# Banded attention and a Mish MLP on one core: VectorE's instructions in program order up to the end of the first product, the first chunk's weight words spread differently, and five buffers for a small store

## The chip, the cores and the metric

The kernel runs on one core of a Trainium2 chip. The metric is the device time of one execution in microseconds (us). Of the kernel before there are three runs: 1056.01 us in the median, from 1054.07 to 1056.55. The engines are TensorE (PE in the profile; PEld is its weight load), VectorE (DVE), ScalarE (ACT), GpSimd (POOL) and SyncE (SP, which only issues transfers). An engine takes its instructions in the order in which they were put into its queue.

## The reference

Two parts follow each other. The first is attention with a band: 8 batches, 8 heads, 576 positions, 64 values per head.

```python
scores = (q @ k.T) / sqrt(64)
bias = slope[h] * -abs(i - j)
mask = (i - j >= 0) and (i - j < 128)
scores = where(mask, scores + bias, -1e9)
attn = exp(scores - max(scores))
attn = attn / (sum(attn) + 1e-9)
x = attn @ v                     # laid out as 4608 tokens x 512
```

The second is an MLP on the 4608 tokens, with `w_in` of 512 x 2048 and `w_out` of 2048 x 512:

```python
h = x @ w_in
g = h * tanh(softplus(h))        # Mish
out = g @ w_out
```

The weights come as 64-bit floats; q, k and v are 32-bit.

## The kernel before

**The MLP.** It works in 9 chunks of 512 tokens (`c` = 0 to 8). Chunk `c` below 8 holds the first 512 positions of batch `c`; chunk 8 holds the last 64 positions of all 8 batches. For each chunk there is a first product and a second product. Both are carried out on numbers split into a high and a low part (`x` into two, the weights into two, `g` into two), with three matmuls for each pair. The first product is `first(c, j)` for `j` = 0 to 7: 24 matmuls with 512 columns into a PSUM tile `h`, and one Mish of ScalarE from `h` into a tile `g` in SBUF. Two successive `j` share one `g` tile, so that a new one is begun at every even `j`. The second product has 32 steps, `second(c, half, j, t)`, of 6 matmuls each; `parts` makes the high part `gh` (ScalarE) and the low part `gl` (GpSimd) of `g` for it.

**The attention.** Attention of batch `c + 1` is woven into the second product of chunk `c`; that of batch 0 comes before everything. For each of 4 pairs of heads there are two units (k = 0 to 7 in all), and beside each even unit a small one for the last 64 positions (`last_unit`, names that end in `l`). A unit goes through these steps, each with a place in the order: `scores` (TensorE, tile `s`), `exps` (VectorE adds the bias and finds the maximum, ScalarE takes the exponential and sums), `fold` (two halves of the band are added, 1e-9 is added to the sum, a reciprocal), `scale` (multiplication with the reciprocal), `weights` (TensorE transposes, VectorE multiplies by a mask and brings the result to SBUF; called the masked copy below), `values` (TensorE, tile `o`), `split_x` (ScalarE makes the high part of `x`, VectorE the low one). The last unit's `values` are copied to `xo` and stored to DRAM until chunk 8.

**The weight words.** `load_w` brings 16 tiles of raw 64-bit words to SBUF (8 of `w_in`, i0 to i7 here, 8 of `w_out`, o0 to o7), each as two halves of 512 words per partition. `convert_w` makes 32-bit numbers of a tile: for each half ScalarE copies into a PSUM tile `t` (named `ti` or `to` in the profile), three VectorE instructions work on `t` and the raw words, then ScalarE copies the high part into a split tile (`si`, `so`) and GpSimd subtracts to get the low part. The PSUM tiles `t` of the two halves lie in the banks `po0` and `po1`, which the second product uses later, or for the tiles made in the second product both in the bank `w`, one after the other; `w` is also the bank of the last unit's transposes (`pt_0l` and so on). Raw tiles, split tiles, the first attention inputs (`first`) and the `g` tiles come from one pool of 20 buffers (`big`). The last tile, o7, is loaded into the buffers of x2 and x3 once the first product of chunk 0 has read them.

**The order.** TensorE's and SyncE's instructions stay in the order in which the program issues them (`InOrder` with `fixed`). The order of VectorE, ScalarE and GpSimd is set ahead of time by a planner that steps through the program with its own costs and picks, for each engine, the earliest instruction of the program that it holds to be ready. So before the change words of the weights stand between the attention's instructions on VectorE, wherever the planner took VectorE to be free. `convert_next` is called three times within attention of batch 0 (at 3.6, 5.6 and 7.6 units), after each `first(0, j)` once or twice, and at every second step of the second product.

Of the kernel before, what the change touches and what calls it, by code (L numbers as in the profile page):

```python
# [8 lines left out]
F32 = mybir.dt.float32  # L9
# [3 lines left out]
AF = mybir.ActivationFunctionType  # L13
ALU = mybir.AluOpType

WINDOW = 128
P = 128
# [24 lines left out]
def attention_mish_mlp(  # L42
# [187 lines left out]
    def unit(b, p, half):  # L230
# [6 lines left out]
        st = {}  # L237
# [35 lines left out]

        def fold():
            sm, pz = st["sm"], st["pz"]
            two = pz if half else pz[:, 1:4:2]
            pool.tensor_tensor(out=two[:, :, :P], in0=two[:, :, :P], in1=two[:, :, P:], op=ALU.add)
            dve.tensor_scalar(out=sm, in0=sm, scalar1=1e-9, scalar2=None, op0=ALU.add)
            dve.reciprocal(sm, sm)

        def scale():
            (pool if b == 0 else dve).tensor_tensor(
                out=st["pz"][:, :, :P], in0=st["pz"][:, :, :P],
                in1=st["sm"].rearrange("p (c n) -> p c n", n=1).to_broadcast([P, 4, P]), op=ALU.mult,
            )

        def weights():
            pz = st["pz"]
# [44 lines left out]
    def last_unit(b, p):  # L333

        st = {}
        name = f"{b}_{p}l"

        def scores():
            qk, z = qkv[(b, p)]

            st["s"] = qkv[("s", b, p)][:, :, :96]
            for i in range(2):
                pe.matmul(
                    st["s"][:, i, :], lhsT=z, rhs=qk[:, 1, 384 + 96 * i : 480 + 96 * i],
                    start=True, stop=True,
                )

        def exps():
            mx = at.tile([P, 1], F32, tag="mxl", name=f"mx{name}")
            sm = st["sm"] = at.tile([P, 1], F32, tag="sml", name=f"sm{name}")  # L350
            pz = st["pz"] = at.tile([P, 192], F32, tag="pzl", name=f"pz{name}")
            dve.tensor_tensor_reduce(
                out=pz.rearrange("p (a n) -> p a n", a=2), in0=st["s"],
                in1=nl[:, p, :].rearrange("p (a n) -> p a n", a=2), scale=-SCALE, scalar=3.0e38,
                op0=ALU.add, op1=ALU.min, accum_out=mx,
            )
            act.activation(pz, pz, AF.Exp, bias=mx, scale=-1.0, accum_out=sm)

        def fold():
            sm, pz = st["sm"], st["pz"]  # L360
            dve.tensor_scalar(out=sm, in0=sm, scalar1=1e-9, scalar2=None, op0=ALU.add)
            dve.reciprocal(sm, sm)
            dve.tensor_tensor(out=pz[:, :64], in0=pz[:, :64], in1=pz[:, P:], op=ALU.add)
            dve.tensor_scalar(out=pz[:, :P], in0=pz[:, :P], scalar1=sm, scalar2=None, op0=ALU.mult)

        def weights():
            t = st["t"] = ps.tile([P, 512], F32, tag="w", name=f"pt{name}")
            pe.transpose(t[:, :P], st["pz"][:, :P], ident)
            pf = st["pf"] = at.tile([P, 2, 2, 64], F32, tag="pfl", name=f"pf{name}", bufs=1)
            shape = [P, 2, 2, 64]  # L370
            dve.tensor_tensor(
                out=pf, in0=t[:, :P].rearrange("p (u i n) -> p u i n", u=1, i=2).to_broadcast(shape),
                in1=masks[:, :, :64].rearrange("p u (i n) -> p u i n", i=1).to_broadcast(shape),
                op=ALU.mult,
            )

        def values():
            va, vl = qkv[("v", b, p)]
            o = st["t"][:, P : P + LEFT]
            for n, val in enumerate((va[:, 3, :], vl)):  # L380
                for i in range(2):
                    pe.matmul(
                        o[HEAD[i]], lhsT=val[:, HEAD[i]], rhs=st["pf"][:, n, i, :],
                        start=(n == 0), stop=(n == 1), skip_group_check=True,
                    )
            xo = at.tile([P, LEFT], F32, tag="xo", name=f"xo{name}")
            dve.tensor_copy(xo, o)
            sp.dma_start(out=xs[p, :, b * LEFT : (b + 1) * LEFT], in_=xo)

        return [  # L390
            (0.01, scores), (0.5, exps), (0.9, fold), (1.4, weights), (1.995, values),
        ]

# [113 lines left out]
        if conv and conv[0] in raw_w:  # L507
            convert_w(*conv.pop(0), tags)

    early = [(k, lambda: convert_next()) for k in (3.6, 5.6, 7.6)]  # L510
    for _, work in sorted(attention(0) + early, key=lambda s: s[0]):
        work()

    for c in range(B + 1):
        for j in range(NJ):
            if c == 0:
                while ("i", j) not in split:
                    convert_next()
            if j == NJ - 1:
                parts(c, 0, 0)  # L520
                parts(c, 0, 1)
            first(c, j)
            if c == 0:
                for _ in range(2 if j > 2 else 1):
                    convert_next()
        if c == 0:
            load_w(*last_w)

        n = 4 * NJ
        steps = []  # L530
        for m in range(2 * NJ):
# [2 lines left out]
            if m >= 2:  # L534
                steps.append((2 * m - 4.1, lambda m=m: parts(c, *divmod(m, NJ))))
            if c == 0:
                steps.append((2 * m + 0.5, lambda: convert_next(("w", "w"))))
        if c + 1 < B:
            steps += [((n - 2) / 9.0 * s - 0.2, f) for s, f in attention(c + 1)]
        elif c + 1 == B:  # L540
# [66 lines left out]
```

## Time and profile before

| what | value |
|---|---|
| median of three runs | 1056.01 us (1054.07 to 1056.55) |
| the profiled execution's own time | 1056.28 us |
| its span, first to last instruction | 1054.5 us |
| mean granted TensorE clock | 0.971 |
| busy: PE, PEld, DVE, ACT, POOL | 998.6, 787.4, 405.7, 391.5, 309.7 us |
| bytes moved | 59.32 MB |

The busy time of an engine is the sum of its instructions' time; for TensorE, whose matmuls are pipelined and whose ends are modelled, it says that there was work, not that it ran at its peak. The granted clock is that of TensorE as a share of 2.4 GHz: 1.00 is that level, 0.50 is 1.2 GHz. Of a timeline's line the columns are: start, duration, engine, operation, output and inputs, shapes, count of merged instructions, and in brackets how long the engine had been idle before and what ended that.

### The profile page before, as it was taken

Reading aid. Unit: us, or ns where it says so; the run is one execution under the profiler, and the core shown is the slowest. Engines: PE = TensorE matmul, PEld = TensorE weight load, DVE = VectorE, ACT = ScalarE, POOL = GpSimd, SP = SyncE. Lnnn points to the kernel's source line nnn. Section 1 sums busy time; section 2 is a strip of 40 time slices with the busy share of each in tenths; the row PEclk is TensorE's granted clock in tenths of the full one; section 3 lists DMA queues with packets and bytes.
Section 4 is the critical chain, followed back from the end, with each engine's and each line's share of the span. In section 5 each row is a group of like instructions: output and inputs, shape, how many; then the busy total and the mean of one; then the engine's idle time right before and its main releaser. Section 6 shows DMA issues by size and latency. Waiting matters only on the chain.

```text
span 1054.5 us, 14241 instructions
## 1 busy us (share of the span) xinstructions
PE 998.6 (95%) x5280; PEld 787.4 (75%) x5280; DVE 405.7 (38%) x1166; ACT 391.5 (37%) x926; POOL 309.7 (29%) x270
## 2 busy tenths in 40 slices
PE   4548989999999999999999999999999999999998
PEld 2336867787778877887778777877787778888886
DVE  4998067502760167106630564037501760000000
ACT  2544554323433345215422443235323442222221
POOL 3513754211431044004410342123311441041032
PEclk9567989999999999999999999999999999999999
DMA  8940022200220023002120032002100201000001
GB/s 269 399 159 13 1 66 91 70 1 20 64 71 32 1 62 93 33 1 60 58 68 1 25 93 68 1 24 85 58 21 1 71 25 41 20 21 21 1 1 40
DMA packets 52133, 59.32 MB, mean 56 GB/s; under 512 B 13024, under 2 KB 32608, under 8 KB 52064
## 3 DMA queue, kind: packets, MB, share of 16 engines
q1 hardware_dynamic: 50880, 57.69, 17.1%
q8 instruction: 42, 0.69, 0.3%
q10 hardware_dynamic: 1184, 0.72, 0.2%
q14 instruction: 27, 0.22, 0.1%
HBM read 47.91 MB, written 10.49 MB: 55 GB/s over the span
## 4 chain that ended last, share of the span: by engine, by line
PE 85%; DMA 4%; DVE 4%; issue 3%; POOL 2%; ACT 1%; SPq 0%; POOLq 0%; DVEq 0%
PE po L30 38%; PE h L30 33%; PE s L30 9%; PE o L30 5%; DMA wi<-in_moe_w_in_dram 2%; DMA wo<-in_moe_w_out_dram 1%; DVE pz L30 1%; POOL si L30 1%; DVE ti L30 1%; POOL so L30 1%; DVE to L30 1%; DMA nb<-in_relb_dram 1%; DVE wi L30 0%; SPq L30 0%; DMA first<-in_k_dram 0%
## 5 line engine op out<-in xcount | busy, mean ns | idle before, releaser
L30 PE MATMUL h<-x,si 128*128 128x512 f32 x1728 | 394.9, 390 | 0.0
L30 PEld LDWEIGHTS h<-x,si 128*128 128x128 f32 x1728 | 325.5, 188 | 68.0 <-issue 0.3
L30 PE MATMUL po<-so,gh 128*128 128x512 f32 x1152 | 324.8, 404 | 0.0
L30 POOL TENSOR_TENSOR gl<-g,gh 128x512 fp32r<-128x512 f32 x144 | 193.6, 1344 | 376.5 <-ACT gh L30 347.0
L30 PEld LDWEIGHTS po<-so,gh 128*128 128x128 f32 x1152 | 207.5, 189 | 48.6 <-ACT x L30 7.0
L30 DVE CUSTOM_DVE_ANT_0 pz<-s,nb 128x256 f32<-128x256 f32 (+1 forms) x256 | 84.6, 386 | 345.6 <-PE s L30 336.0
L30 PE MATMUL po<-so,gl 128*128 128x512 f32 x576 | 178.7, 391 | 0.0
L30 ACT ACTIVATE g<-h 128x1024 f32<-128x1024 f32 x72 | 74.0, 1028 | 268.8 <-PE h L30 268.8
L30 ACT ACTIVATE pz<-pz,mx 128x256 f32<-128x256 f32 (+1 forms) x256 | 120.3, 471 | 118.0 <-DVE mx L30 117.9
L30 POOL TENSOR_TENSOR pz<-pz 128x256 f32<-128x256 f32 x64 | 64.8, 1013 | 314.9 <-PE po L30 174.0
L30 ACT ACTIVATE gh<-g 128x512 fp32r<-128x512 f32 x144 | 90.6, 629 | 116.6 <-PE po L30 112.4
L30 PEld LDWEIGHTS po<-so,gl 128*128 128x128 f32 x576 | 108.6, 188 | 24.2
L30 DVE TENSOR_TENSOR pz<-s,masks 128x1024 f32<-128x1024 f32 x64 | 78.2, 1222 | 29.2 <-PE s L30 29.2
L30 DVE TENSOR_TENSOR pz<-pz,sm 128x512 f32<-128x512 f32 x56 | 61.9, 1106 | 11.0 <-POOL pz L30 8.9
L30 DVE COPY ob<-po 128x512 f32<-128x512 f32 x18 | 12.4, 692 | 124.9 <-PE po L30 124.9
L30 PE MATMUL s<-qk 64*128 64x128 f32 (+1 forms) x448 | 57.7, 376 | 0.0
L30 PE MATMUL o<-pz,va 128*64 128x128 f32 (+1 forms) x560 | 54.9, 325 | 0.0
L30 PEld LDWEIGHTS o<-pz,va 128*64 128x64 f32 x560 | 33.3, 136 | 27.8 <-issue 10.2
L30 ACT ACTIVATE x<-o 128x512 fp32r<-128x512 f32 x32 | 19.1, 598 | 83.8 <-PE o L30 83.8
L30 PE MATMUL o<-pz,first 128*64 128x128 f32 (+1 forms) x80 | 14.1, 517 | 36.0 <-DVE pz L30 36.0
L30 PE MATMUL s<-ident,pz 128*128 128x128 f32 x256 | 41.1, 286 | 7.4 <-POOL pz L30 4.3
L30 ACT ACTIVATION_READ_ACCUMULATOR pz<-pz,mx 128x1 f32 x256 | 47.8, 187 | 0.0
(114 smaller groups left out, 556.9 us busy)
## 6 DMA issues: line engine op xcount, KB each, us to landing
wi<-in_moe_w_in_dram SPq DMA_DIRECT2D x16, 512.0 KB, 10.4
wo<-in_moe_w_out_dram SPq DMA_DIRECT2D x16, 512.0 KB, 10.8
out_dram<-ob SPq DMA_DIRECT2D x32, 256.0 KB, 2.0
qk<-in_q_dram SPq DMA_DIRECT2D x28, 288.0 KB, 3.7
qk<-in_k_dram SPq DMA_DIRECT2D x28, 288.0 KB, 3.7
va<-in_v_dram SPq DMA_DIRECT2D x28, 256.0 KB, 2.9
first<-in_q_dram SPq DMA_DIRECT2D x4, 288.0 KB, 3.9
first<-in_k_dram SPq DMA_DIRECT2D x4, 288.0 KB, 4.4
```

Of the source, the lines that this page charges most:

```text
L30: ins = method(*args, **kwargs)
```

## The change

VectorE's instructions are kept in program order from the start until the first product of chunk 0 is issued (`dve.fixed`). Of the words of the weights only i0 is made within attention of batch 0 (at 7.0 units); after each `first(0, j)` two tiles are made as long as more than four are left, and the last four (o4 to o7) in the second product of chunk 0, at every step's half instead of every second one's. In all chunks `1e-9` is added by ScalarE. From batch 1 on `fold` and `scale` of a unit become one VectorE instruction for each column block with two halves (two in an even unit, four in an odd one), with a minimum's accumulator that nobody reads, and one ScalarE copy with a scale for each block with one half; GpSimd and the wide VectorE multiplication are no longer used there. In the last unit the addition and the multiplication of the first 64 columns become one VectorE instruction, and ScalarE scales the other 64. `xo` gets five buffers instead of two.

```diff
--- before.py
+++ after.py
@@ -273,16 +273,30 @@
 
         def fold():
             sm, pz = st["sm"], st["pz"]
-            two = pz if half else pz[:, 1:4:2]
-            pool.tensor_tensor(out=two[:, :, :P], in0=two[:, :, :P], in1=two[:, :, P:], op=ALU.add)
-            dve.tensor_scalar(out=sm, in0=sm, scalar1=1e-9, scalar2=None, op0=ALU.add)
+            if b == 0:
+                two = pz if half else pz[:, 1:4:2]
+                pool.tensor_tensor(out=two[:, :, :P], in0=two[:, :, :P], in1=two[:, :, P:], op=ALU.add)
+            act.activation(sm, sm, AF.Copy, bias=1e-9)
             dve.reciprocal(sm, sm)
 
         def scale():
-            (pool if b == 0 else dve).tensor_tensor(
-                out=st["pz"][:, :, :P], in0=st["pz"][:, :, :P],
-                in1=st["sm"].rearrange("p (c n) -> p c n", n=1).to_broadcast([P, 4, P]), op=ALU.mult,
-            )
+            sm, pz = st["sm"], st["pz"]
+            if b == 0:
+                pool.tensor_tensor(
+                    out=pz[:, :, :P], in0=pz[:, :, :P],
+                    in1=sm.rearrange("p (c n) -> p c n", n=1).to_broadcast([P, 4, P]), op=ALU.mult,
+                )
+                return
+
+            unread = at.tile([P, 4], F32, tag="un", name=f"un{name}")
+            for c in range(4):
+                if half or c % 2:
+                    dve.tensor_tensor_reduce(
+                        out=pz[:, c, :P], in0=pz[:, c, :P], in1=pz[:, c, P:], scale=sm[:, c : c + 1],
+                        scalar=3.0e38, op0=ALU.add, op1=ALU.min, accum_out=unread[:, c : c + 1],
+                    )
+                else:
+                    act.activation(pz[:, c, :P], pz[:, c, :P], AF.Copy, scale=sm[:, c : c + 1])
 
         def weights():
             pz = st["pz"]
@@ -358,10 +372,14 @@
 
         def fold():
             sm, pz = st["sm"], st["pz"]
-            dve.tensor_scalar(out=sm, in0=sm, scalar1=1e-9, scalar2=None, op0=ALU.add)
+            act.activation(sm, sm, AF.Copy, bias=1e-9)
             dve.reciprocal(sm, sm)
-            dve.tensor_tensor(out=pz[:, :64], in0=pz[:, :64], in1=pz[:, P:], op=ALU.add)
-            dve.tensor_scalar(out=pz[:, :P], in0=pz[:, :P], scalar1=sm, scalar2=None, op0=ALU.mult)
+            un = at.tile([P, 1], F32, tag="unl", name=f"un{name}")
+            dve.tensor_tensor_reduce(
+                out=pz[:, :64], in0=pz[:, :64], in1=pz[:, P:], scale=sm, scalar=3.0e38,
+                op0=ALU.add, op1=ALU.min, accum_out=un,
+            )
+            act.activation(pz[:, 64:P], pz[:, 64:P], AF.Copy, scale=sm)
 
         def weights():
             t = st["t"] = ps.tile([P, 512], F32, tag="w", name=f"pt{name}")
@@ -383,7 +401,7 @@
                         o[HEAD[i]], lhsT=val[:, HEAD[i]], rhs=st["pf"][:, n, i, :],
                         start=(n == 0), stop=(n == 1), skip_group_check=True,
                     )
-            xo = at.tile([P, LEFT], F32, tag="xo", name=f"xo{name}")
+            xo = at.tile([P, LEFT], F32, tag="xo", name=f"xo{name}", bufs=5)
             dve.tensor_copy(xo, o)
             sp.dma_start(out=xs[p, :, b * LEFT : (b + 1) * LEFT], in_=xo)
 
@@ -507,8 +525,9 @@
         if conv and conv[0] in raw_w:
             convert_w(*conv.pop(0), tags)
 
-    early = [(k, lambda: convert_next()) for k in (3.6, 5.6, 7.6)]
-    for _, work in sorted(attention(0) + early, key=lambda s: s[0]):
+
+    dve.fixed = True
+    for _, work in sorted(attention(0) + [(7.0, convert_next)], key=lambda s: s[0]):
         work()
 
     for c in range(B + 1):
@@ -521,10 +540,12 @@
                 parts(c, 0, 1)
             first(c, j)
             if c == 0:
-                for _ in range(2 if j > 2 else 1):
-                    convert_next()
+                for _ in range(2):
+                    if len(conv) > 4:
+                        convert_next()
         if c == 0:
             load_w(*last_w)
+            dve.fixed = False
 
         n = 4 * NJ
         steps = []
@@ -534,7 +555,7 @@
             if m >= 2:
                 steps.append((2 * m - 4.1, lambda m=m: parts(c, *divmod(m, NJ))))
             if c == 0:
-                steps.append((2 * m + 0.5, lambda: convert_next(("w", "w"))))
+                steps.append((m + 0.5, lambda: convert_next(("w", "w"))))
         if c + 1 < B:
             steps += [((n - 2) / 9.0 * s - 0.2, f) for s, f in attention(c + 1)]
         elif c + 1 == B:
```

## Rows read from the trace of the kernel before

**Rows 1.** Busy time by stage: start:end, length, engines, granted clock, DMA share, GB/s.

```profile
16.40:88.03 71.63, 34.84 (x204) 23.38 (x204) 66.28 (x169) 33.24 (x88) 22.01 (x20) 0.64 0.70 254
88.03:133.45 45.42, 45.42 (x194) 37.20 (x192) 13.08 (x22) 25.79 (x39) 29.54 (x24) 0.96 0.00 1
133.45:208.46 75.01, 70.75 (x422) 53.64 (x422) 49.81 (x140) 34.12 (x99) 33.25 (x27) 0.95 0.23 73
208.46:319.70 111.24, 111.24 (x614) 87.57 (x613) 44.22 (x134) 41.59 (x104) 29.66 (x24) 1.00 0.15 45
```

**Rows 2.** The chain of work that ended last: start, duration, what.

```profile
208.46 43.52 PE h L30 x192
...
1006.42 43.53 PE po L30 x192
```

**Rows 3.** TensorE's waits up to 135 us: total, times, longest.

```profile
PE o L30 <- DVE pz L30: 36.0, 8, 8.7
```

**Rows 4.** Timeline of TensorE in attention of batch 0 and behind it.

```profile
16.37 1.55 PE L30 MATMUL o<-pz,first 128*64 128x256 f32 x8 [1.26 <-DVE pz L30]
...
29.66 1.98 PE L30 MATMUL o<-pz,first 128*64 128x128 f32 x12 [8.65 <-DVE pz L30]
...
34.07 0.27 PE L30 MATMUL pt_1l<-ident,pz_1l 128*128 128x128 f32 x1
39.00 1.55 PE L30 MATMUL o<-pz,first 128*64 128x256 f32 x8 [4.66 <-DVE pz L30]
...
43.57 1.11 PE L30 MATMUL s<-ident,pz 128*128 128x128 f32 x4
...
88.03 45.49 PE L30 MATMUL h<-x,si 128*128 128x512 f32 x192
```

**Rows 5.** Timeline of VectorE up to the end of the first product.

```profile
28.40 1.21 DVE L30 TENSOR_TENSOR pz<-s,masks 128x1024 f32<-128x1024 f32 x1
...
91.80 1.30 DVE L30 TENSOR_SCALAR to<-to 128x512 uint32<-128x512 uint32 x2
...
94.20 1.28 DVE L30 SCALAR_TENSOR_TENSOR wo<-wo,to 128x512 uint32<-128x512 uint32 x2
```

**Rows 6.** Timeline of ScalarE: the first word, and the first product.

```profile
21.99 0.62 ACT L30 ACTIVATE ti<-wi 128x512 f32<-128x512 f32 x1 [5.74 <-DMA wi<-in_moe_w_in_dram]
...
95.48 1.03 ACT L30 ACTIVATE g<-h 128x1024 f32<-128x1024 f32 x1 [1.85 <-PE h L30]
96.40 2.31 ACT L30 ACTIVATE si<-wi 128x512 fp32r<-128x512 f32 x4
...
107.28 3.44 ACT L30 ACTIVATE si<-wi 128x512 fp32r<-128x512 f32 x6
```

**Rows 7.** Timeline of SyncE's queue: the first store of xo.

```profile
51.99 0.33 SPq L30 DMA_DIRECT2D xs<-xo_0l  x1
```

**Rows 8.** Timeline of GpSimd in the first product.

```profile
97.13 5.14 POOL L30 TENSOR_TENSOR si<-wi,si 128x512 fp32r<-128x512 f32 x4 [14.16 <-ACT si L30]
```

**Rows 9.** Timeline of ScalarE at the start of the second product.

```profile
136.38 0.62 ACT L30 ACTIVATE to<-wo 128x512 f32<-128x512 f32 x1 [1.65 <-DMA wo<-in_moe_w_out_dram]
```

**Rows 10.** Timeline of VectorE there: the last instruction of either half of o7.

```profile
138.50 0.69 DVE L30 SCALAR_TENSOR_TENSOR wo<-wo,to 128x512 uint32<-128x512 uint32 x1
...
147.67 0.68 DVE L30 SCALAR_TENSOR_TENSOR wo<-wo,to 128x512 uint32<-128x512 uint32 x1
```

**Rows 11.** Timeline of TensorE there.

```profile
146.26 1.09 PE L30 MATMUL s<-ident,pz 128*128 128x128 f32 x4 [3.12 <-DVE pz L30]
148.50 0.45 PE L30 MATMUL pt_0l<-ident,pz_0l 128*128 128x128 f32 x1 [1.14 <-DVE wo L30]
```

**Rows 12.** Timeline of VectorE in a later chunk: the multiplication of an odd unit.

```profile
375.57 1.45 DVE L30 TENSOR_TENSOR pz<-pz,sm 128x512 f32<-128x512 f32 x1
```

**Rows 13.** Timeline of TensorE there: the transposes of that unit.

```profile
379.90 0.60 PE L30 MATMUL s<-ident,pz 128*128 128x128 f32 x4
```

**Rows 14.** Busy time and granted clock behind a burst of TensorE (columns as in Rows 1).

```profile
54.00:56.00 2.00, 0.62 (x5) 0.38 (x3) 2.00 (x4) 0.56 (x1) 0.00 (x0) 0.98 1.01 404
```

## Prediction, made before the change was run

> **What bounds the kernel now.** I read the busy time by stage first, then the chain of waits, then TensorE's waits and the timelines of the first 210 us. From 208.46 us, where the first product of chunk 1 begins, TensorE is busy without a gap: 111.24 of 111.24 us in one whole chunk at clock 1.00 [rows 1], and the chain runs over TensorE's lines to the last product at 1006.42 [rows 2]. The change takes no matmul away, so these 1054.5 - 208.46 = 846.0 us stay as long as nothing makes TensorE wait there. What can move is the first 208.46 us, in three stages [rows 1]: attention of batch 0 (to 88.03; VectorE busy 66.28 of 71.63 us, TensorE 34.84, clock 0.64), the first product (45.42 us, TensorE full), and the second product with attention of batch 1 (75.01 us, against 111.24 - 43.52 = 67.7 us in a later chunk). In the first stage TensorE waits 36.0 us in 8 waits for VectorE's masked copies [rows 3]: its queue is a burst of `values`, `scores` and transposes of some 5 us, then nothing while VectorE works on weight words.
>
> **Attention of batch 0, words moved out.** In program order VectorE has only attention to do, so a masked copy follows as soon as the transposes are there. A burst lasts from 29.66 to 34.34 = 4.68 us behind an odd unit and from 39.00 to 44.68 = 5.68 us behind an even one [rows 4]; the masked copy adds 1.26 us until the next `values` (28.40 to 29.66) [rows 4, 5]. The cycles are 5.94 and 6.94 us where they now take about 10. From the first `values` at 16.37 [rows 4], four even and three odd cycles without the last one's scores: unit 6's `values` start at 16.37 + 3 x 6.94 + 3 x 5.94 = 55.0; 1.55 + 0.64 of those, 1.11 of transposes and 1.26 of masked copy give 59.5, unit 7's `values` (1.98) 61.5 us. Two things are added. The word i0 stands in unit 7's place on VectorE: 91.80 to 95.48 is 3.68 us for a tile [rows 5]; it lies mostly beside TensorE's burst, so 0 to 3.7 us, I take 1.5, as the burst is the longer. And ScalarE may take i0's copy when its data is not there yet, as it does now (5.74 us until 21.99) [rows 6]; the exponentials of unit 2 would stand behind it: 0 to 3.5 us, taken as 1. That is 64 us at the low clock of these rows. With all bursts at 1.00, half as long, the same sum gives about 51. One burst ended at 0.98 [rows 14], but the stage's mean was 0.64 [rows 1]; with pauses of 1.3 us in place of 5 it will be higher. I take 60: 28 us earlier than 88.03.
>
> The five `xo` buffers belong to this step: the first store leaves SyncE's queue only at 51.99, behind the weight loads [rows 7], and with two buffers the third copy to `xo`, now due near 40 us, would hold VectorE until then. I count the buffers as the removal of that wait and nothing more. SyncE's queue keeps its order.
>
> **The first product.** 192 matmuls, 45.42 us now [rows 1]. VectorE has 11 tiles behind attention, 11 x 3.68 = 40.5 us [rows 5], so it keeps ahead of 24 matmuls per 5.4 us on the whole. But only i0 is ready at the start. ScalarE's copies into split tiles come in groups behind every second Mish (96.40 behind 95.48, and six at 107.28) [rows 6], not when VectorE is done: buffers of a pool are handed out in program order, and `g` stands before the next split tiles. Before, three words were made ahead; after, i1 must wait for the first Mish. From the start of the product to that Mish 7.45 us, to the copy 0.92, to GpSimd 0.73, and 1.28 for a half [rows 4, 6, 8]: the low part of i1's first half is there after 10.4 us, of its second after 11.7, while TensorE is through with i0 at about 7.4 and can do 2 and then 4 more matmuls of 0.23. It waits 2.5 + 0.4 = 2.9 us; with 0.7 for the clock the stage is 49.0 us (bounds 43.5, all at 1.00 and no wait, and 52). It ends at 109.0 instead of 133.45.
>
> **The second product of chunk 0.** Here four tiles instead of one are made, in the one bank `w`, half behind half. A half takes 136.38 to 139.19 = 2.81 us from ScalarE's copy to VectorE's last instruction [rows 9, 10]. By the same program order the first small transposes `pt_0l` get the bank only behind all eight halves. VectorE ends its fixed list some 45 us after the product's start (1.3 for the last x, 40.5, and 3 of holds by ScalarE), 4 us before the second product; 8 x 2.81 = 22.5 us later, and 2 more for attention's own instructions between, the bank is free: 20.5 us into the second product. TensorE reaches `pt_0l` after 146.26 - 3.12 - 133.45 + 1.09 = 10.8 us [rows 1, 11]. It waits 9.7 us. Waits of 4.26 us cost 75.01 - 67.7 = 7.3 us before [rows 1, 11], so 3.0 of them were the low clock behind the wait; I add the same. Second product: 67.7 + 9.7 + 3.0 = 80.4 us (bounds: 67.7 if words are made early in VectorE's gaps, 91 with VectorE and ScalarE in turns). Chunk 1 starts at 189.4 instead of 208.46.
>
> **The cheaper fold and scale, and ScalarE's additions, in later chunks.** An odd unit's multiplication ends at 377.02 and its transposes start at 379.90 [rows 12, 13]: 2.9 us to spare. The new VectorE instruction with a scalar operand is not in the trace; four of them lie between a small part of 1.45 us and four times 1.45 [rows 12], I take 1.5 in all, since they read half the data each and one addition goes. ScalarE's added pieces are each under the 0.62 us of a 512-wide copy [rows 9]. GpSimd's addition before them goes. So 0 in either direction, hidden by TensorE's own work; if the 2.9 us were used up, the transposes would wait for the rest.
>
> **Sum.** 60 + 49.0 + 80.4 + 846.0 = 1035.4 us of span; the profiled execution took 1056.28 - 1054.5 = 1.78 us more than its span, so 1037.2 us. It lies 0.27 above the median of the runs, within their spread.
>
> **Rivals.** *The clock rises in attention of batch 0.* With pauses of 1.3 us the bursts run at 1.00 from the third on: the stage ends at 53, the first product takes 43.5 + 3, the second 80.4, chunk 1 starts at 179.9: 1027.7 us. For it speaks the 0.98 at the end of a burst [rows 14], against it that most bursts of the same length stayed low [rows 1]. The Trainium skill (TensorE: Matmul & The Clock Gate, Part 1) says that the throttled state is the default and that activity releases it; by that rule this rival is the likelier end of the range, and the trace agrees in that 1.00 stands in the later, gapless chunks.
>
> *Slower: the words in `w` hold TensorE far longer.* The two halves of o7 took from 136.38 to 148.35, 12.0 us, as attention's instructions got between them on VectorE [rows 9, 10]: 6.0 us per half. Eight at that pace end 43.9 us into the second product, TensorE waits 33.1 us, the stage takes 103.8 and chunk 1 starts at 212.8: 1060.6 us. It decides against the change from 5.4 us per half on. For it speaks that row; against it that TensorE, once it waits, brings VectorE no new attention work.
>
> *The change does not do what it says.* If ScalarE's or GpSimd's order, not VectorE's words, sets the 10 us cycle, attention ends at 88 as now and the added waits remain: 88 + 49.0 + 80.4 is 217.4, 1065 us. Against it: 66.28 of 71.63 us of VectorE are busy [rows 1].
>
> *Later chunks become bound by attention.* Four new instructions in a row that each wait for a GpSimd subtraction (1.28) [rows 8] cost 5.1 us, 2.2 beyond the 2.9 to spare, four times in each of 7 chunks: 62 us, 1099. From 0.7 us per odd unit on the gain is gone. Against it: GpSimd has 16 subtractions in a chunk, spaced by several us, so one or two can hit. The Trainium skill (SBUF — State Buffer, Who interferes with whom) says that a VectorE instruction with two SBUF inputs and a GpSimd instruction that reads SBUF exclude each other for their whole length; the 1.45 us in rows 12 are in line with it.
>
> **Chances.** Forecast 0.56 (its own range 1030 to 1045), clock 0.27, slow words 0.09, no release 0.05, later chunks 0.03. The range 1023 to 1048 leaves out the slower rivals and the far ends of the two stages' bounds. About 0.3% (3.2 us) is what can be told from no change: faster 0.85 (the first two and the near part of the third), same 0.03, slower 0.12.
>
> **What would show it.** Right: `h` starts near 60 us; VectorE has no weight word before unit 7; one wait of TensorE of some 3 us for GpSimd's `si` behind the first 24 matmuls; one of 5 to 15 us before `pt_0l`, released by VectorE's last word; the second product of chunk 1 as long as before. Wrong: `h` later than 70 us, more than one wait in the first product, or any wait of TensorE in later chunks.

## The result, and the profile after

The changed kernel takes 1043.57 us (median of 4, 1042.77 to 1045.11) where the kernel before took 1055.62 on the same chip: ratio 0.9889, 95% interval 0.9872 to 0.9907. It is faster, 12 us in the median; the forecast was 1037.2 us. The profiled execution has a span of 1043.4 us (before 1054.5) at a mean clock of 0.978.

Busy time by stage of the changed kernel, with the columns of [rows 1]: attention of batch 0, first product, second product with attention of batch 1, and chunk 1 as a whole.

```profile
16.48:65.61 49.13, 30.66 (x203) 21.22 (x204) 30.16 (x97) 22.64 (x78) 17.07 (x16) 0.77 0.98 363
65.61:122.39 56.78, 51.06 (x194) 40.36 (x193) 52.68 (x82) 36.96 (x58) 31.27 (x24) 0.87 0.02 6
122.39:197.18 74.79, 70.17 (x422) 53.09 (x421) 46.47 (x168) 41.73 (x127) 28.40 (x22) 0.95 0.24 73
197.18:308.57 111.39, 111.39 (x614) 87.72 (x613) 42.46 (x162) 46.52 (x128) 21.00 (x16) 1.00 0.15 44
```

Against [rows 1]: `h` starts 22.4 us earlier (65.61, before 88.03), the first product is 11.4 us longer (56.78, before 45.42), and the second and a later chunk are unchanged within 0.1 us. That is the 11.1 us of the span. (The 208.46 of [rows 1] and [rows 2], at which chunk 1 was taken to start, is a step of the chain of work; TensorE's timeline of the kernel before has the first `h` of chunk 1 at 208.30. The stages below go by the timelines; by them the last window above ends 0.16 us into chunk 2.) VectorE's load has moved from the first row (66.28 busy before, 30.16 now) to the second (13.08 before, 52.68 of 56.78 now).

TensorE's waits up to 100 us (total, times, longest); the line answers to [rows 3]:

```profile
PE o L30 <- DVE pz L30: 17.6, 8, 4.7
```

And its waits from 65 us to the start of chunk 1:

```profile
PE pt_0l L30 <- DVE wo L30: 3.9, 1, 3.9
PE h L30 <- ACT g L30: 3.4, 1, 3.4
PE h L30 <- ACT si L30: 1.7, 1, 1.7
PE s L30 <- ACT pz L30: 0.8, 1, 0.8
PE h L30 <- POOL si L30: 0.7, 1, 0.7
```

The second line was not forecast: in the first product TensorE waits for a Mish (`g`). The timeline of TensorE has it at 108.53, and the wait that answers to the second of [rows 11] at 137.55:

```profile
75.10 0.73 PE L30 MATMUL h<-x,si 128*128 128x512 f32 x2 [1.67 <-ACT si L30]
76.49 28.65 PE L30 MATMUL h<-x,si 128*128 128x512 f32 x118 [0.65 <-POOL si L30]
108.53 13.93 PE L30 MATMUL h<-x,si 128*128 128x512 f32 x48 [3.40 <-ACT g L30]
137.55 0.45 PE L30 MATMUL pt_0l<-ident,pz_0l 128*128 128x128 f32 x1 [3.87 <-DVE wo L30]
```

### The profile page after: what moved, and what is told of

It reads as the page before. It is cut to its first block, busy times and chain, and to the rows that moved or that the text cites. A ratio compares the mean times of both kernels' runs of the same rounds, so it can differ in the third digit from the quotient of the medians.

```text
span 1043.4 us, 14406 instructions
## 1 busy us (share of the span) xinstructions
PE 999.6 (96%) x5280; PEld 788.0 (76%) x5280; DVE 395.1 (38%) x1350; ACT 429.9 (41%) x1110; POOL 249.6 (24%) x214
## 4 chain that ended last, share of the span: by engine, by line
PE 89%; DMA 5%; DVE 2%; issue 1%; SPq 1%; ACT 1%; POOL 0%; POOLq 0%; DVEq 0%; ACTq 0%
PE po L30 38%; PE h L30 36%; PE s L30 9%; PE o L30 5%; DMA wi<-in_moe_w_in_dram 2%; DMA wo<-in_moe_w_out_dram 1%; SPq L30 1%; DMA xs<-xo_1l 1%; DVE ti L30 1%; DMA nb<-in_relb_dram 1%; DVE to L30 0%; PE pt_0l L30 0%; DVE wo L30 0%; PE pt_1l L30 0%; PE pt_3l L30 0%
## 5 line engine op out<-in xcount | busy, mean ns | idle before, releaser
L30 PE MATMUL h<-x,si 128*128 128x512 f32 x1728 | 400.6, 394 | 5.7 <-ACT g L30 3.4
L30 POOL TENSOR_TENSOR gl<-g,gh 128x512 fp32r<-128x512 f32 x144 | 188.1, 1307 | 709.5 <-ACT gh L30 682.1
L30 DVE CUSTOM_DVE_ANT_0 pz<-pz,sm 128x128 f32<-128x128 f32 x168 | 78.3, 511 | 1.2
L30 DVE TENSOR_TENSOR x<-o,x 128x512 fp32r<-128x512 f32 x32 | 22.1, 691 | 60.8 <-ACT x L30 60.8
L30 PEld LDWEIGHTS s<-ident,pz 128*128 128x128 f32 x256 | 32.6, 146 | 15.2 <-POOL pz L30 6.0
```

Source lines behind the costliest of these rows:

```text
L30: ins = method(*args, **kwargs)
```

## The experiments

Stages in us, read from one profiled execution of each kernel; ratio to the kernel before on the same chip, with its 95% interval. Several chips were used, on which the kernel before took 1055.03 to 1055.89 us in the median, so that medians of different rows compare to about 1 us. The code cuts leave out lines, at `...` and around them.

| kernel | median | ratio | `h` starts | first product | second product | chunk 1 starts |
|---|---|---|---|---|---|---|
| before | 1055.62 | 1 | 88.03 | 45.42 | 74.9 | 208.3 |
| after | 1043.57 | 0.9889 [0.9872, 0.9907] | 65.61 | 56.78 | 74.8 | 197.2 |
| order_only | 1046.77 | 0.9911 [0.9896, 0.9926] | 67.83 | 56.81 | 74.2 | 198.9 |
| fold_only | 1053.39 | 0.9980 [0.9970, 0.9989] | 84.75 | 45.37 | 74.9 | 205.0 |
| xo2 | 1055.39 | 0.9996 [0.9987, 1.0006] | 80.04 | 54.29 | 74.5 | 208.8 |
| words_held | 1057.97 | 1.0015 [1.0006, 1.0025] | 67.77 | 49.86 | 93.8 | 211.5 |
| held_13 | 1048.03 | 0.9932 [0.9915, 0.9948] | 66.10 | 54.13 | 81.7 | 201.9 |
| two_early | 1047.21 | 0.9921 [0.9907, 0.9936] | 67.30 | 54.25 | 77.0 | 198.5 |
| one_ahead | 1050.32 | 0.9954 [0.9939, 0.9968] | 67.27 | 58.34 | 77.2 | 202.8 |
| best | 1039.92 | 0.9859 [0.9844, 0.9874] | 67.08 | 56.38 | 69.2 | 192.7 |
| counts | 1044.66 | 0.9890 [0.9875, 0.9905] | 68.60 | 45.33 | 84.1 | 198.1 |
| best_pairs | 1052.32 | 0.9961 [0.9945, 0.9976] | 66.34 | 68.92 | 69.6 | 204.9 |
| tuned | 1051.26 | 0.9957 [0.9945, 0.9969] | 65.23 | 53.27 | 83.5 | 202.0 |
| last | 1038.27 | 0.9837 [0.9823, 0.9850] | 67.86 | 44.32 | 77.6 | 189.8 |

### The parts of the change: order_only, fold_only, xo2

order_only is the changed kernel with the old fold and scale; fold_only is the kernel before with the new ones.

```diff
-            act.activation(sm, sm, AF.Copy, bias=1e-9)
+            dve.tensor_scalar(out=sm, in0=sm, scalar1=1e-9, scalar2=None, op0=ALU.add)
...
-            for c in range(4):
...
+            (pool if b == 0 else dve).tensor_tensor(
```

> The changed kernel (1043.6 us) with fold, scale and the last unit's fold as they were before: only VectorE's order, the placing of the weight words and the five buffers are left of the change. Theory, the gain is all in the first 210 us and comes from the order: 1043.6, within 3 us, and every later chunk at 111.2 us. Rival, the cheaper fold and scale are part of the gain (GpSimd's addition and a 1.1 us multiplication per unit less): 1047 to 1053, with waits of TensorE in later chunks or a second product of chunk 0 that is longer by more than 3 us.

> The kernel before with the new fold, scale and last unit's fold alone (VectorE free to be ordered by the planner, words as before, two xo buffers). Theory, these parts are hidden in the later chunks and shorten only the chain of batch 0 by some 0.3 us per unit, which VectorE's words hide: within 2.5 us of before, 1053 to 1058 us. Rival, they are 2 to 3 us of the gain, as the difference of the run without them (1046.8) hints: 1050 to 1053 us.

Between before and fold_only lie 1.6 us in the medians (1055.03 on the same chip) and 3.3 us in the start of `h`. Between order_only and after lie 3.2 and 2.2 us, but their intervals overlap, and kernels with the same attention as the changed kernel's start `h` anywhere from 65.61 to 68.60 us (a table on this stands in the section on the prediction). The two of them with order_only's granted clock in that stage, 0.67, start it at 67.08 and 67.27, 0.6 to 0.8 us ahead of order_only. So the new fold gains something in attention of batch 0 (the last units' part and ScalarE's additions, as only these are new there), how much is not settled, and it changes nothing in later chunks, where neither kernel shows a wait of TensorE.

xo2 is the changed kernel with two `xo` buffers as before.

```diff
-            xo = at.tile([P, LEFT], F32, tag="xo", name=f"xo{name}", bufs=5)
+            xo = at.tile([P, LEFT], F32, tag="xo", name=f"xo{name}")
```

> The changed kernel with two buffers for xo in place of five. Theory, the buffers are a condition of the order: VectorE in program order reaches the third copy to xo near 45 us, but the first store is issued only near 52 us behind the weight loads and lands some 5 us later, so VectorE stands until 57 us, the first product starts near 77 us instead of 65.6, and the kernel takes 1053 to 1056 us. Rival, the store is early enough or VectorE has that time to spare: 1043 to 1045 us.

The whole gain is gone. The rows are from three timelines of xo2: SyncE issues the store of the first small copy at 52.21; VectorE's third small copy is held by that store, not until it is issued but until it has landed, 9 us later; and TensorE waits for the masked copy behind it.

```profile
52.21 0.33 SPq L30 DMA_DIRECT2D xs<-xo_0l  x1
```

```profile
61.37 0.22 DVE L30 COPY xo_2l<-pt_2l 128x64 f32<-128x64 f32 x1 [16.00 <-DMA xs<-xo_0l]
```

```profile
63.91 1.97 PE L30 MATMUL o<-pz,first 128*64 128x128 f32 x12 [13.42 <-DVE pz L30]
```

In program order nothing can pass the waiting copy. So the order needs the buffers; the two edits are one. (The buffers without the order were not run. In the kernel before, the planner has the third copy at 64.60, and it waits for nothing.)

### The four words beside the second product: words_held, held_13

In the changed kernel o4 to o7 are not in VectorE's fixed order, so the planner may put them earlier, and it did. The timeline of VectorE behind attention of batch 0 has halves of o4 to o6 (`to`, `wo`) from 61.58 on, in turn with those of i1 to i5 (`ti`, `wi`):

```profile
61.58 0.70 DVE L30 TENSOR_SCALAR to<-to 128x512 uint32<-128x512 uint32 x1 [0.70 <-ACT to L30]
...
67.62 0.69 DVE L30 TENSOR_SCALAR ti<-ti 128x512 uint32<-128x512 uint32 x1
68.21 0.68 DVE L30 SCALAR_TENSOR_TENSOR wo<-wo,to 128x512 uint32<-128x512 uint32 x1
...
91.28 0.68 DVE L30 SCALAR_TENSOR_TENSOR wo<-wo,to 128x512 uint32<-128x512 uint32 x1
```

words_held keeps them where the program has them; held_13 is words_held with o4 and o5 made in the first product.

```diff
-                steps.append((m + 0.5, lambda: convert_next(("w", "w"))))
+                def held():
+                    dve.fixed = True
+                    convert_next(("w", "w"))
+                    dve.fixed = False
+                steps.append((m + 0.5, held))
```

```diff
-                    if len(conv) > 4:
+                    if len(conv) > 2:
```

> The changed kernel, but o4 to o7, made in the second product, are also in program order on VectorE, so that the planner can't put them between the words of the first product. Theory A, o4 to o6 between i1 to i5 made the first product long (56.8 us): it falls to about 49 us, no wait for Mish; instead pt_0l waits some 16 us and the second product takes 85 to 89 us: 1043 to 1047 us in all. Rival B, ScalarE's order is late in the first product whatever VectorE's list holds: first product still 55 to 58 us, second product 85 us: 1050 to 1054 us.

> All words in VectorE's program order (as in words_held, 1058.0 us), but two more tiles (o4, o5) are made in the first product, so that o6 and o7 alone pass through the bank w. Theory, pt_0l waits for every half that stands before it in w: with 4 halves in place of 8 its wait of 23.6 us falls by 4 x 2.8 to 4 x 4 us, to 7 to 12 us; first product 50 to 52 us, 1042 to 1047 us in all. Rival, the wait is one for VectorE's whole list and not for the bank: it stays above 18 us, 1053 us or more.

In words_held the first product is 49.86 us with no wait for a Mish, and the price appears at `pt_0l`; the row is from its timeline of TensorE:

```profile
151.35 0.45 PE L30 MATMUL pt_0l<-ident,pz_0l 128*128 128x128 f32 x1 [23.58 <-DVE wo L30]
```

The bank `w` is handed on slowly: the last five of the eight halves follow each other with nothing of attention between them, 3.4 us apart, of which 1.3 are VectorE's wait for ScalarE's next `to` (timeline of VectorE):

```profile
142.21 0.70 DVE L30 TENSOR_SCALAR to<-to 128x512 uint32<-128x512 uint32 x1 [1.30 <-ACT to L30]
...
145.60 0.70 DVE L30 TENSOR_SCALAR to<-to 128x512 uint32<-128x512 uint32 x1 [1.24 <-ACT to L30]
```

Theory A was right on the first product; the second was 5 us longer than it had, and the time 11 us above its range. So the planner's freedom, which I had counted only as a lower bound of the second product, is worth some 14 us (1057.97 to 1043.57). held_13 shows 8.05 us at `pt_0l` with two words fewer, as expected, and 3.43 us for a Mish again at the end of its first product, which takes 54.13 us and not 50 to 52; it ends 1 us above what was expected.

### i1 earlier: two_early, one_ahead

```diff
-    for _, work in sorted(attention(0) + [(7.0, convert_next)], key=lambda s: s[0]):
+    for _, work in sorted(attention(0) + [(4.0, convert_next), (6.0, convert_next)], key=lambda s: s[0]):
```

```diff
-                while ("i", j) not in split:
+                while ("i", min(j + 1, NJ - 1)) not in split:
```

> The changed kernel with two words made inside attention of batch 0, i0 at 4.0 and i1 at 6.0 units (where VectorE waits 2.4 and 1.8 us for scores), instead of i0 at 7.0. Theory, the wait behind the first 24 matmuls (1.7 + 0.7 us, and the low clock behind it) comes from having one word ahead: attention ends at 65 to 67 us, that wait is gone, the first product takes 51 to 53 us, 1038 to 1041 us in all. Rival, VectorE and ScalarE are the pace of the first product, so the wait only moves: 1043 to 1045 us, with a longer wait for Mish or for a later word.

> The changed kernel (1043.6 us) where i1, too, is issued ahead of first(0, 0) in the program, so that its split tile is handed out before the first g; VectorE's list stays as it is. Theory, the wait behind the first 24 matmuls (1.7 + 0.7 us) is due to the order in which the buffers are handed out: it is gone, with some 2 us of low clock behind it; first product 52 to 54 us, 1039 to 1041 us in all. Rival, as with two words ahead, ScalarE's late Mish takes the place of it: that wait grows from 3.4 to 6 us or more, 1043 to 1046 us.

Both take the forecast wait for i1 away or shorten it (2.3 us to none, and to 1.5), and both are slower than after, two_early by so little that the intervals meet. The next wait grows; rows of two_early, then of one_ahead, from their timelines of TensorE:

```profile
108.87 12.75 PE L30 MATMUL h<-x,si 128*128 128x512 f32 x48 [6.75 <-ACT g L30]
```

```profile
95.64 12.81 PE L30 MATMUL h<-x,si 128*128 128x512 f32 x48 [3.36 <-ACT g L30]
112.92 12.77 PE L30 MATMUL h<-x,si 128*128 128x512 f32 x48 [4.47 <-ACT g L30]
```

That alone does not make two_early slower: its first product is 2.5 us shorter than after's. Its `h` starts 1.7 us later and its second product is 2.2 us longer; there both kernels wait 5.27 us at `pt_0l`, a wait that VectorE's `sm` ends, where a word ends after's 3.87.

### Why a Mish comes late: best, counts

The Mish of `j` = 4 begins a new `g` tile. In the changed kernel's timeline of ScalarE it starts at 107.48, right behind a split copy (`so`) of a word of o0, although TensorE was through with its `h` tile long before (the one of `j` = 3 started at 94.29, and a product takes 5.4 us):

```profile
94.29 1.03 ACT L30 ACTIVATE g<-h 128x1024 f32<-128x1024 f32 x1 [2.29 <-PE h L30]
95.22 0.65 ACT L30 ACTIVATE si<-wi 128x512 fp32r<-128x512 f32 x1
...
106.91 0.66 ACT L30 ACTIVATE so<-wo 128x512 fp32r<-128x512 f32 x1 [0.94 <-POOL si L30]
107.48 1.00 ACT L30 ACTIVATE g<-h 128x1024 f32<-128x1024 f32 x1
```

best puts all words in VectorE's order, i1 before the first product, o0 to o5 in it, o6 before and o7 behind `pt_0l`. counts differs from best in one line: one and two tiles behind the products in turn, where best has two behind each until it has no more.

```diff
-                while ("i", j) not in split:
+                while ("i", min(j + 1, NJ - 1)) not in split:
...
-                    if len(conv) > 4:
+                    if len(conv) > 2:
...
+                if m < 2:
+                    steps.append(((0.5, 6.5)[m], held))
```

```diff
-                for _ in range(2):
+                for _ in range(1 + j % 2):
```

> All words in VectorE's program order; i1 issued ahead of first(0, 0); o0 to o5 made in the first product; o6 at 0.5 and o7 at 6.5 in the second, the latter behind pt_0l in the bank w. Theory: attention ends near 67 us as in words_held, the first product takes 46 to 49 us (no wait behind the first 24 matmuls, none for Mish), pt_0l waits at most 4 us, the second product takes 69 to 74 us: 1030 to 1036 us in all. Rival, o7 then comes too late for its matmuls or holds pt_1l: a wait of 5 us or more there, 1038 to 1043 us.

> Theory: a Mish that begins a new g tile is late because that tile's buffer is handed out in program order, behind the split tiles of all words that the program has issued ahead of it, and these wait for VectorE. With one and two words behind the products in turn (1, 2, 1, 2, ...) in place of two each, the program runs less far ahead of VectorE: no wait of TensorE for a Mish above 1 us in the first product (best: 5.71 and 3.96), which is then 45 to 50 us long (best: 56.4); VectorE's list, 13 tiles of some 4.1 us, then sets when the second product can begin. 1034 to 1038 us. Rival (the planner's own order of ScalarE's copies makes the Mish late, whatever the number of words): the waits for the Mish stay at 5 us or more in sum, and the time at 1040.

best is 3.7 us faster than after in the medians (the two intervals just meet), by what its second product gains; the short first product that was expected of it did not come, with 5.71 and 3.96 us of waits for a Mish. In counts these are gone: the first product takes 45.33 us without a wait. The pool hands out its buffers in program order, so a `g` tile stands behind the split tiles of all words that the program has issued before it, and those wait for VectorE; fewer words ahead, and the Mish is in time. The timelines of ScalarE bear this out against the rival that the planner merely orders ScalarE badly. The Mish of `j` = 4, which begins a tile, comes right behind the first split copy of the last word issued before it in each of these kernels: o0 in after, words_held and held_13, o1 in best, two_early and one_ahead, i7 in counts. The Mish of `j` = 3, which begins none, passes the words before it: in the rows above it stands at 94.29, ahead of the first split copy of i5 at 95.22. The time expected did not follow: the row is from counts' timeline of TensorE in the second product.

```profile
130.24 2.07 PE L30 MATMUL po<-so,gh 128*128 128x512 f32 x4 [14.77 <-DVE wo L30]
```

The bank `po` there comes free only when VectorE is done with the words that are made in it, 13 tiles behind attention. The late Mish had hidden a shortage that is VectorE's own.

### The pace of VectorE's words: best_pairs, tuned

In program order the three instructions of a half follow each other and each needs the one before. In the changed kernel's timeline of VectorE that is a step of 0.73, 0.73 and 0.60 us, 2.06 for a half and 4.1 for a tile, where two instructions of different halves (the x2 rows of [rows 5]) stand 0.60 apart:

```profile
98.48 0.69 DVE L30 TENSOR_SCALAR ti<-ti 128x512 uint32<-128x512 uint32 x1
99.21 0.70 DVE L30 SCALAR_TENSOR_TENSOR ti<-wi,ti 128x512 uint32<-128x512 uint32 x1
99.94 0.69 DVE L30 SCALAR_TENSOR_TENSOR wi<-wi,ti 128x512 uint32<-128x512 uint32 x1
100.55 0.69 DVE L30 TENSOR_SCALAR ti<-ti 128x512 uint32<-128x512 uint32 x1
```

best_pairs is best with the halves of a tile in alternation; tuned has that and the turns of counts, with o5 to o7 in the second product.

```diff
-        for a, raw in enumerate(halves):
-            ... all steps of a half
+        for group in raws:
+            ... each step for both halves, then the next
```

> As best, but the three VectorE instructions of a tile's two halves alternate, where the halves lie in two banks. Theory (in strict order each of the three waits for the one before it, 2.06 us per half; in alternation 0.60 us each, 3.68 per tile): VectorE is through its list some 4 us earlier, the late Mish comes earlier by as much, the first product is 50 to 53 us long (best: 56.4), 1033 to 1037 us. Rival (the Mish waits for buffers and for ScalarE, not for VectorE's pace): the waits stay, 1039 to 1041 us.

> Both edits, 1 and 2 words in turn and the two halves of a tile in alternation, and three tiles of w_out in place of two within the second product, two of them at its very start through the banks w and o. If both theories hold, attention of batch 0 ends at 67 us as in best, the first product is 45.5 to 47 us long with no wait above 1 us, the second 69 to 72 us: 1027 to 1031 us. Rival (two early tiles in the second product hold TensorE at o or at the small transposes): a wait of 4 us or more there, 1034 us or more.

Both theories fell, and best_pairs is slower than best by 12.4 us in the medians; TensorE's waits for a Mish are 2.77, 8.93 and 7.82 us in it, against 5.71 and 3.96 in best. Its timeline of VectorE shows why: a tile now takes 77.20 to 82.11, 4.9 us.

```profile
77.20 0.70 DVE L30 TENSOR_SCALAR ti<-ti 128x512 uint32<-128x512 uint32 x1 [1.01 <-ACT ti L30]
78.30 0.70 DVE L30 TENSOR_SCALAR ti<-ti 128x512 uint32<-128x512 uint32 x1 [0.40 <-ACT ti L30]
78.91 1.28 DVE L30 SCALAR_TENSOR_TENSOR ti<-wi,ti 128x512 uint32<-128x512 uint32 x2
80.10 1.28 DVE L30 SCALAR_TENSOR_TENSOR wi<-wi,ti 128x512 uint32<-128x512 uint32 x2
82.11 0.70 DVE L30 TENSOR_SCALAR ti<-ti 128x512 uint32<-128x512 uint32 x1 [0.73 <-ACT ti L30]
```

The instructions are close together, but both banks now end together, and VectorE waits for ScalarE's split copy and next `ti` of each. With one half after the other ScalarE fills one bank while VectorE works in the other. tuned, whose VectorE works in the same way, waits 2.63 and 5.38 us for a Mish and 12.14 us for a word in the second product.

### Fewer words behind attention: last

The edit against counts: i0 and i1 within attention of batch 0, o5 to o7 in the second product, two of them through the banks `w` and `o`.

```diff
-    for _, work in sorted(attention(0) + [(7.0, convert_next)], key=lambda s: s[0]):
+    for _, work in sorted(attention(0) + [(4.0, convert_next), (6.0, convert_next)], key=lambda s: s[0]):
...
-                    if len(conv) > 2:
+                    if len(conv) > 3:
...
+                    at_step = (0.2, 0.7, 6.5)[m]
+                    tags = ("w", "w") if m == 2 else ("w", "o")
```

> counts (one and two tiles in turn, halves one after the other) with less for VectorE to do behind attention: i0 and i1 both within attention of batch 0, where VectorE is idle for 23.7 of 52.2 us, and o5 to o7 in the second product. Theory (in counts and in best TensorE waits for the number of words that VectorE has to make behind attention, 13 tiles of 4.1 us against a first product of 45.3 us, wherever the wait shows): with 11 tiles VectorE's list ends some 47 us behind the start of the first product; first product 45.3 to 47 us, no wait for a Mish above 1 us, a wait of 3 to 6 us for a word in the second product instead of 14.8, chunk 1 begins at 186 to 189, 1033 to 1036 us. Rival (the waits are set by the turns that VectorE and ScalarE take over a bank, whatever the number of words): a wait of 9 us or more for a word in the second product, 1039 us or more.

The first product is 44.32 us, the shortest of all, and the 14.77 us have become 3.96 and 2.20 (timeline of TensorE):

```profile
117.68 2.07 PE L30 MATMUL po<-so,gh 128*128 128x512 f32 x4 [3.96 <-DVE wo L30]
122.81 2.07 PE L30 MATMUL po<-so,gh 128*128 128x512 f32 x4 [2.20 <-DVE wo L30]
```

The theory came out, with its sizes somewhat off: the waits are 6.2 us together, chunk 1 starts 0.8 us later and the time is 2.3 us above what was expected. At 1038.27 us it has the lowest median of the kernels here; its interval lies below that of the changed kernel and overlaps that of best. What stays open is the share of each of its edits: the number of tiles behind attention (13 in counts, 11 here) was not varied alone, as the banks of two tiles in the second product changed with it.

## Why the prediction was right in its sign and off in its terms

The sum was 60 + 49.0 + 80.4 + 846.0 = 1035.4 us of span; measured are 65.6 + 56.8 + 74.8 + 846.2 = 1043.4. The errors are +5.6, +7.8, -5.6 and +0.2. The last is none: by the timeline that the measured figure goes by, the kernel before has 1054.5 - 208.30 = 846.2 too. That the second and the third nearly cancel is luck: both come from words that moved from one stage to the other, which the prediction did not foresee. The sign, too, rests on that move: with the words where the forecast had them (words_held) the ratio is 1.0015.

**Attention of batch 0 (60, measured 65.6).** The sum of the cycles seems right: unit 5's `values` were due at 16.37 + 3 x 6.94 + 2 x 5.94 = 49.1 and start at 49.47. That is luck. The forecast cycles stand for the low clock; the first three steps from `values` to `values` are 7.09, 7.00 and 7.09 us where it has 6.94 and 5.94 in turn, and the next two, with faster bursts, 5.38 and 6.43. The step that failed is "a masked copy follows as soon as the transposes are there". In program order the next unit's `exps` stand before it on VectorE. Rows of the changed kernel, first from TensorE's timeline, then from VectorE's, where the masked copy at 41.77 comes behind `exps` that begin at 40.40, as the transposes end:

```profile
39.74 0.65 PE L30 MATMUL s<-ident,pz 128*128 128x128 f32 x4
...
43.04 1.55 PE L30 MATMUL o<-pz,first 128*64 128x256 f32 x8 [2.54 <-DVE pz L30]
```

```profile
40.40 0.41 DVE L30 CUSTOM_DVE_ANT_0 pz<-s,nb 128x256 f32<-128x256 f32 x1
...
41.77 1.22 DVE L30 TENSOR_TENSOR pz<-s,masks 128x1024 f32<-128x1024 f32 x1
```

TensorE waits 1.28 to 2.54 us for a masked copy, and 4.69 behind i0 (17.6 in 8), where I had 1.26. Two sizes were off besides. The word i0, taken at 1.5 us, holds VectorE from 51.27 to 55.39, and unit 6's `values` start 9.16 us behind unit 5's in place of 5.94: 3.2, near the upper bound. And I took 4 us off for a higher clock. It did rise, from 0.64 to 0.77, and TensorE's busy time fell from 34.84 to 30.66 us. What that is worth shows in kernels whose attention of batch 0 has the same instructions as the changed kernel's (their edits concern what comes behind it; none sets the clock by itself); the columns are read from 16.4 us to the start of `h`:

| kernel | granted clock | TensorE busy | `h` starts |
|---|---|---|---|
| after | 0.77 | 30.66 | 65.61 |
| held_13 | 0.74 | 31.95 | 66.10 |
| best | 0.67 | 32.39 | 67.08 |
| one_ahead | 0.67 | 32.58 | 67.27 |
| words_held | 0.60 | 35.52 | 67.77 |
| counts | 0.57 | 36.12 | 68.60 |

From 0.57 to 0.77 the stage ends 3.0 us earlier, so that of the 4 us some 2 were there (an estimate from this table, for 0.64 to 0.77). By the rule of the Trainium skill (TensorE: Matmul & The Clock Gate, Part 1) cited in the prediction, activity releases the clock; the trace agrees in the clock, and the stage's end follows it, but by less than TensorE's busy time does. The rival that the stage would end at 53 is out. (The "about 51" for all bursts at 1.00 is a slip: halving the 36.4 us of bursts in the 64 gives 46.) The hold that I feared of ScalarE is there once, for i0's second half at 22.90, with unit 2's exponentials behind it at 23.46; no run shows what it costs.

**The five `xo` buffers.** The wait that they remove is there as the step said, but it does not end with the store's issue at 52 us: it ends when the store has landed, at 61.37 in xo2. Its size is 11.8 us in the median.

**The first product (49.0, measured 56.8).** The step on i1 held: 1.67 + 0.65 = 2.3 us of wait, 2.9 forecast, behind the first Mish (73.47) as described. The step that failed is "so it keeps ahead of 24 matmuls per 5.4 us on the whole". VectorE had not 11 tiles to make but 14, as the planner drew o4 to o6 forward, and a tile that stands alone in program order takes 4.1 us, not 3.68; it was busy for 52.68 of 56.78 us. With the 11 tiles of the forecast (words_held) the first product takes 49.86 us, near the 49.0, though a tile takes 4.1 us there too; so the other 7 us go with the three tiles drawn forward. I had seen that buffers come in program order and used it for i1, but not for the `g` tile of `j` = 4, which stands behind the split tiles of more words than VectorE had made: 3.4 us. counts, and the place of that Mish in each kernel, show the cause. Of the 56.8 us, 43.5 are the matmuls at full clock, 5.7 the three waits, and the other 7.5 are put down to low clock behind the start and the waits. Busy time and clock of three stretches of the changed kernel show this (columns of [rows 1]):

```profile
65.61:70.50 4.89, 4.89 (x14) 3.89 (x13) 4.76 (x8) 1.51 (x4) 0.00 (x0) 0.55 0.24 62
...
80.00:108.00 28.00, 25.13 (x110) 20.41 (x109) 26.38 (x42) 19.23 (x31) 17.54 (x15) 0.99 0.00 1
108.00:114.00 6.00, 5.47 (x13) 4.31 (x14) 5.62 (x10) 4.98 (x9) 3.56 (x3) 0.50 0.00 0
```

The granted clock is 0.99 up to the wait of 3.40 us and 0.50 behind it: the wait costs more than its own length. I had allowed 0.7 us for it.

**The second product of chunk 0 (80.4, measured 74.8).** The mechanism is there, the wait at `pt_0l` for VectorE's last word in `w`, at 3.87 us in place of 9.7. The step that failed is that all eight halves would come behind VectorE's fixed list: the planner drew six of them forward, nearly all into the first product. The prediction had words made early as the lower bound of this stage and not as a load on the one before. Where they are kept in place (words_held) the wait is 23.58 us, well above the forecast too: eight halves end 33.7 us behind the stage's start, 4.2 each (3.4 where nothing lies between them), between the 2.81 of the forecast and the 6.0 of the slower rival. With the eight halves where the forecast had them, words_held takes 1057.97 us and is no faster than the kernel before.

**Fold, scale and later chunks (0, measured 0).** Chunk 1 takes 111.2 us before and after by TensorE's timelines (208.30 to 319.54, and 197.18 to 308.41), with no wait of TensorE. What I left out is that ScalarE's additions and the last unit's new instruction shorten attention of batch 0: 3.3 us by fold_only, where the planner also orders VectorE anew, under 1 us by order_only at like clock.

The unforecast wait in the first product was named as a sign that would make the prediction wrong ("more than one wait in the first product"), and it did show in that term. The wait at `pt_0l` lay below the 5 to 15 us that were named as a sign of being right.

## What to carry to other kernels

When an engine is put in program order, list what every one of its instructions may wait for, buffers of other engines' stores included: here two buffers in place of five took the whole gain away. And list what stands before each instruction in the new order: the masked copy comes behind work of the next unit. Where a pool hands out buffers in program order, issuing work early does not make it early; it puts every tile of the pool that is issued behind it, whichever engine fills it, behind the first write of that work. A wait that goes only pays if the engine behind it has time left: count its instructions at the pace that they have in the new order, and see where the rest will be waited for. And where the clock of TensorE differs from kernel to kernel, compare a stage's length only at like clock.

## What the runs showed of the hardware

In these traces a VectorE instruction that needs the result of the one just before it starts 0.73 us after it, against 0.60 for one that does not (512 words of 32 bits per partition, rows above). And the new fold's 128-wide instruction takes 0.35 us alone but four times as long beside a GpSimd subtraction; rows of the changed kernel in chunk 1, first VectorE's timeline, then GpSimd's:

```profile
252.71 0.35 DVE L30 CUSTOM_DVE_ANT_0 pz<-pz,sm 128x128 f32<-128x128 f32 x1
252.98 1.37 DVE L30 CUSTOM_DVE_ANT_0 pz<-pz,sm 128x128 f32<-128x128 f32 x1
254.28 0.34 DVE L30 CUSTOM_DVE_ANT_0 pz<-pz,sm 128x128 f32<-128x128 f32 x1
```

```profile
252.77 1.43 POOL L30 TENSOR_TENSOR gl<-g,gh 128x512 fp32r<-128x512 f32 x1 [3.31 <-ACT gh L30]
```

The Trainium skill (SBUF — State Buffer, Who interferes with whom) states this exclusion, and the trace agrees: the second instruction ends 0.15 us behind the subtraction. In chunk 1 at most one of a unit's two or four is hit; that is 1.0 us, under the 2.9 us to spare, and the rival's four in a row do not occur there.
